# Window attention and two MLPs on one core: zeros beside the keys cleared by GpSimd behind the last token, queries copied by ScalarE alone, and another order of the first loads and the first work

## The chip, the cores and the metric

The kernel runs on one core of a Trainium2 chip. The metric is the time on the device in microseconds, as the median of several runs. A core has TensorE (PE: matrix products, with the loading of its weights, PEld, beside it), VectorE (DVE), ScalarE (ACT), GpSimd (POOL) and SyncE (SP), which here issues all DMAs. Every engine works through its own instructions in order. A lower-case q behind an engine's name means its queue or sequencer.

## The reference, cut to what matters

Attention over a window of 16 tokens to each side and, beside it, over one summary per block of 32 tokens (maximum of the keys, mean of the values), then two MLPs one behind the other. Batch 2, 8 heads, 768 tokens, 64 values a head; 1536 rows of 512, inner width 2048; all in float32.

```python
k_sum = k.reshape(B, H, nb, block, D).max(axis=3)
v_sum = v.reshape(B, H, nb, block, D).mean(axis=3)
scores_l = scale * np.matmul(q, k.transpose(0, 1, 3, 2))
mask_l = np.abs(pos[:, None] - pos[None, :]) < window
scores_s = scale * np.einsum('bhsd,bhnd->bhsn', q, k_sum) + np.log(block)
a = softmax(concat([where(mask_l, scores_l, -1e9), scores_s]))
attn = np.matmul(a, concat([v, v_sum]))
x = attn.transpose(0, 2, 1, 3).reshape(B * S, H * D)
h = np.maximum(x @ w_in, 0.0); x = h * h @ w_out
h = x @ w_in2; g = P(h) / (Q(h) + 1e-6)          # P cubic, Q quadratic in |h|
out = g @ w_out2
```

## The kernel before

The MLPs bound most of the kernel. Every float32 number is split into a high and a low part, and each product is three matmuls (lines 525 and 612). There are four passes over the tokens; the first takes five of the sixteen column groups of the first MLP, 256 tokens at a time, and attention for later tokens is laid between its matmuls. A weight tile goes through four steps: a load into one of three buffers, then w_top on ScalarE, w_dec on VectorE (two instructions, lines 130 and 131) and w_put on ScalarE and GpSimd (lines 144 and 145). A buffer's next load waits for w_dec.

Attention works on units d: a pair of heads times 128 tokens of two 64-token windows each, 24 in all, four pairs per 256 tokens. The keys of a pair are loaded with 8 tokens on each of 96 partitions, 2 KB a piece. [...] k_rel brings the two heads together, k_tr transposes eight pieces on TensorE into two PSUM banks of four pieces each, k_lin copies each bank into the order of windows, k_put takes the maxima of blocks.

The work up to the sixth unit is written out by hand in START, and each engine runs its part of that in the order of the list, while loads (LOADS) and constants (build_consts) are placed by the framework's scheduler: an instruction that must wait can fall behind later ones. A letter is a step, its digit the pair or unit:

- R, A: k_rel on VectorE or ScalarE. t: k_tr. l and k: k_lin of the first and the second bank, on ScalarE and VectorE. c: maxima and their copy to the first four windows. C, B: their copy to the other windows, on VectorE or ScalarE.
- q: transposes of the queries. z: their copy out of PSUM (line 398), half a pair on ScalarE and half on VectorE. s: scores. m: mask and maximum. e: exponentials. r: sums. n: division on GpSimd. p: transposes. b, f: copy out of PSUM on ScalarE or VectorE. o: product with the values. x, y: high and low part of the result.
- S, V, u, w: block means of the values. T, D, W: w_top, w_dec, w_put. X: matmuls for nothing but warmth.

In LOADS, k are the keys of a pair, q and Q queries, v values by token for the block means, n values by window, and w weight tiles. When START is over, the main loop begins, whose first product is at line 525 (h).

Of the kernel before, what the change touches and what calls it, by code (L numbers as in the profile page):

```python
# [16 lines left out]


LOADS = (
    "q0 k0 k1 k2 k3 n2 w0 v0 v1 q1 v2 v3 n0 w1 Q1 w2 n1 n3"  # L20
)
START = (
# [4 lines left out]
)  # L27


# [1 line left out]
def tile_window_attention_moe_moe(  # L31
# [13 lines left out]
    nc = tc.nc  # L45
    B, H, S, D = q.shape
    NT, DM = out.shape
    DFF = w_in1.shape[1]
    P = 128
    BLK, WIN = 32, 16  # L50
# [100 lines left out]
    ap = actx.enter_context(tc.tile_pool(name="ap", bufs=2))  # L151
    TR = 8
    VP = S // TR
    KP = VP + 2 * WIN // TR
    K0 = WIN // TR
    bw = ap.tile([VP, HK], F32, name="bw", bufs=1)
    qz = [ap.tile([P, 4, 2, LO], F32, name=f"qz{j}", bufs=1) for j in range(2)]
    kss = [ap.tile([P, NB], F32, name=f"kss{j}", bufs=1) for j in range(NP)]
# [5 lines left out]
    early = [wp.tile([P, 2 * DM], F32, tag=("wh", "wl")[j % 2], name="early") for j in range(14)]  # L164
# [7 lines left out]
    ]  # L172
    kst = const.tile([P, TR, 4, D], F32, tag="xh2", name="kst")[0:KP]
    vst = const.tile([P, 4, TR, D], F32, tag="xl2", name="vst")[0:VP]
    ksrc = {}
# [3 lines left out]
    def bank(name):  # L179

        tag = banks.pop(0)
        t = (ps_a if tag[0] == "a" else ps_y).tile([P, 512], F32, tag=tag, name=name)
        held[id(t)] = tag
        return t
# [3 lines left out]
    def free(t):  # L188

        banks.append(held.pop(id(t)))  # L190
# [4 lines left out]

    def build_consts():
        make_identity(nc, ident)
        for z in qz:
            nc.vector.memset(z[0:D, :, 1], 0.0)
            nc.vector.memset(z[D:P, :, 0], 0.0)  # L200
        for t in prs:
            nc.vector.memset(t[:, :, HK:], 1e-9)
        m = mk[0:LO, 1, 0:WT]
        nc.vector.memset(m, 0.0)
        nc.gpsimd.affine_select(
            out=m, in_=m, pattern=[[1, WT]], compare_op=ALU.is_ge, fill=NEG, base=-1,
            channel_multiplier=-1,
        )
        nc.gpsimd.affine_select(
            out=m, in_=m, pattern=[[-1, WT]], compare_op=ALU.is_ge, fill=NEG, base=2 * WIN - 1,  # L210
            channel_multiplier=1,
        )
        nc.vector.memset(mk[:, :, WT:], math.log(BLK))
        nc.vector.tensor_copy(mk[LO:P, 1, 0:WT], m)
        m = mk[:, 1:2, 0:WT]
        nc.vector.tensor_copy(mk[:, 0:1, 0:WT], m)
        nc.vector.tensor_copy(mk[:, 2:6, 0:WT], m.to_broadcast([P, 4, WT]))
        nc.vector.memset(mk[:, 0, 0:WIN], NEG)
        nc.vector.memset(mk[:, 5, WT - WIN:WT], NEG)
        nc.vector.memset(bw, 1.0 / BLK)  # L220
        for sgn, base in ((1, 0), (-1, BLK - 1)):
            nc.gpsimd.affine_select(
                out=bw[:, WT:], in_=bw[:, WT:], pattern=[[-sgn * BLK, NB]],
                compare_op=ALU.is_ge, fill=0.0, base=base - (sgn < 0) * (TR - 1),
                channel_multiplier=sgn * TR,
            )
        nc.vector.memset(bw[:, 0:WT], 0.0)
# [12 lines left out]
    def rows(src, h, n, t):  # L240
        return src[h:h + n].rearrange("h (p r) d -> p h (r d)", r=t)

    def e_load(p):

        t = early[p][0:KP].rearrange("p (h r d) -> p h r d", r=TR, d=D)
        nc.sync.dma_start(
            out=t[K0:K0 + VP].rearrange("p h r d -> p h (r d)"), in_=rows(k[0], 2 * p, 2, TR)
        )
        ksrc[p] = t

    def k_rel(p, copy):

        t = early[4 + p][0:KP].rearrange("p (r h d) -> p r h d", r=TR, d=D)
        copy(out=t.rearrange("p r h d -> p h r d"), in_=ksrc[p])
        ksrc[p] = t

    def k_load(hh):

        for h in range(4):
            late(nc.sync.dma_start(  # L260
                out=kst[K0:K0 + VP, :, h], in_=k[1, 4 * hh + h].rearrange("(p r) d -> p r d", r=TR)
            ))
        for j in range(2):
            ksrc[2 * hh + j] = kst[:, :, 2 * j:2 * j + 2]

    def s_load(bb, h, t):

        n = t.shape[1]
        x = nc.sync.dma_start(
            out=t.rearrange("p h r d -> p h (r d)"), in_=rows(v[bb], h, n, TR)  # L270
        )
        if bb:
            late(x)
        for j in range(n // 2):
            vsrc[h // 2 + j] = t[:, 2 * j:2 * j + 2]
# [14 lines left out]
    def q_load(g, hs=slice(0, H)):  # L290

        bb, i, _, _ = at(g * 2 * NP)
        for j in range(2):
            x = nc.sync.dma_start(
                out=qr[g % 2][:, j, hs],
                in_=q[bb, hs, (i + j) * P:(i + j + 1) * P].rearrange("h p d -> p h d"),
            )
            if g > 1:
                late(x)
# [20 lines left out]
    pk = {}  # L320

    def k_tr(p):

        src = ksrc[p].rearrange("p r h d -> p r (h d)")
        pk[p] = [bank("pk"), bank("pk")]
        for r in range(TR):
            pt = pk[p][r // 4]
            nc.tensor.transpose(
                out=pt[:, r % 4 * KP:(r % 4 + 1) * KP], in_=src[:, r],
                identity=ident[0:KP, 0:KP],  # L330
            )

    def k_lin(p, b, copy):

        pt = pk[p][b]
        src = pt[:, 0:4 * KP]
        src = bass.AP(src.tensor, src.offset, [
            list(src.ap[0]), [LO // TR, NWIN], [1, WT // TR], [KP, 4],
        ])
        dst = kt[p][:, :, 0:WT].rearrange("p w (t r) -> p w t r", r=TR)  # L340
        copy(out=dst[:, :, :, 4 * b:4 * b + 4], in_=src)
        free(pt)

    def k_put(p, wins=slice(0, NWIN), copy=nc.vector.tensor_copy, first=True):

        ks = kss[p]
        if first:
            nc.vector.tensor_reduce(
                out=ks.rearrange("p (w n) -> p w n", n=2),
                in_=kt[p][:, :, WIN:WIN + LO].rearrange("p w (n t) -> p w n t", t=BLK),  # L350
                axis=AX.X, op=ALU.max,
            )
        dst = kt[p][:, wins, WT:]
        copy(
            out=dst, in_=ks.rearrange("p (o n) -> p o n", o=1).to_broadcast([P, dst.shape[1], NB])
        )
# [35 lines left out]
    def d_z(d):  # L392


        pt = pq.pop(d)
        for e, mul in enumerate((nc.scalar.mul, nc.vector.tensor_scalar_mul)):
            r = slice(e * D, (e + 1) * D)
            mul(
                qz[d % 2][r, :, e], pt[r, 0:2 * P].rearrange("p (c t) -> p c t", t=LO), 1.0 / SC
            )  # L400
        free(pt)
# [13 lines left out]
    def d_m(d):  # L415
# [11 lines left out]
        )  # L427
        nc.vector.tensor_reduce(out=mx[:, 0:4], in_=s, axis=AX.X, op=ALU.max, negate=True)
        free(pt)
# [8 lines left out]
    def d_r(d):  # L438
        mx, pr = ex.pop(d)
        rs = ap.tile([P, 4], F32, tag="rs", name="rs", bufs=2)  # L440
        nc.vector.tensor_reduce(out=mx[:, 4:8], in_=pr, axis=AX.X, op=ALU.add)
        nc.vector.reciprocal(out=rs, in_=mx[:, 4:8])  # L442
# [17 lines left out]
    def d_b(d, copy=nc.scalar.copy):  # L460
        pp = ap.tile([HK, 4, 2, LO], F32, tag="pp", name="pp", bufs=2)
        copy(out=pp.rearrange("p c e t -> p (c e t)"), in_=po[d][0:HK])
        free(po[d])
        po[d] = pp
# [189 lines left out]
    S0 = 8  # L654
# [45 lines left out]

    nc.scalar.preload_act_table_set("natural_log_exp_and_others")
    hh = [slice(0, H // 2), slice(H // 2, H)]
    v0 = []

    def v_early(p):
        v0.append(early[8 + p][0:VP].rearrange("p (h r d) -> p h r d", r=TR, d=D))
        s_load(0, 2 * p, v0[p])

    loads = dict(
        k=e_load, q=lambda j: q_load(0, hh[j]), Q=q_load, v=v_early,  # L710
        n=lambda i: v_load(0, *divmod(i, 2)), w=lambda i: w_load(*divmod(i, 2)),
    )

    for t in [*early[0:4], kst]:
        nc.vector.memset(t[0:K0], 0.0)
        nc.vector.memset(t[VP:KP], 0.0)
    for x in LOADS.split():
        loads[x[0]](int(x[1:]))
    NL = LOADS.count("w")
# [16 lines left out]
    def w_next(j):  # L736
        k = wq[j]
        (w_top, w_dec, w_put)[j](*divmod(k, 2))
        wq[j] += 1
        if j == 1 and k + NL < NW:  # L740
            w_load(*divmod(k + NL, 2))
# [24 lines left out]
    dve, act = nc.vector.tensor_copy, nc.scalar.copy  # L766
# [3 lines left out]
    def v_last(h, copy):  # L770
        v_put(h, 1, copy)
        free(pvs.pop(h))

    parts = dict(
        X=warm, R=lambda p: k_rel(p, dve), A=lambda p: k_rel(p, act), t=k_tr,
        l=lambda p: k_lin(p, 0, act), k=lambda p: k_lin(p, 1, dve),
        c=lambda p: k_put(p, some, dve),
        C=lambda p: k_put(p, rest, dve, False), B=lambda p: k_put(p, rest, act, False), q=d_t, z=d_z, s=d_s, m=d_m, e=d_e,
        r=d_r, n=d_n, p=d_p, b=d_b, f=lambda d: d_b(d, dve), o=d_o, x=d_x, y=d_y,
        S=lambda p: s_add(v0[p], LEFT), V=lambda h: v_sum(h, LEFT),  # L780
        u=lambda h: v_put(h, 0, act), w=lambda h: v_last(h, act), T=lambda i: w_next(0),
        D=lambda i: w_next(1), W=lambda i: w_next(2),
# [124 lines left out]
```

## Time and profile before

| | |
|---|---|
| median of 3 runs | 653.3 us (651.43 to 655.62) |
| the profiled execution | 650.38 us, span 648.6 us |
| TensorE busy | 610.7 us, 94% of the span |
| VectorE, ScalarE, GpSimd busy | 426.4, 402.8, 351.0 us |
| weight loads of TensorE | 519.4 us |
| DMA | 51.47 MB, mean 79 GB/s |
| granted TensorE clock, mean | 0.995 |

Times are microseconds from the start of the span. An engine's share of the span is an average over stages that have different limits: the first work has little for TensorE to do, and from some 57 us on TensorE hardly rests. A view by stretches of time tells these apart.

### The profile page before, as it was taken

What the parts mean: (1) busy time and instruction counts of PE and PEld (TensorE: products, weight loads), DVE (VectorE), ACT (ScalarE), POOL (GpSimd) and SP (SyncE); (2) the same over time, 40 slices, a digit from 0 to 9 for tenths busy, and PEclk for the clock granted to TensorE, in tenths of its full rate; (3) what the DMA queues carried; (4) which work ended last, traced back from release to release, by engine and by line L of the source; (5) the groups of instructions that cost most, each with busy time, mean ns of one, the idle gap of its engine ahead of it and who ended that gap; (6) DMA issues with size and microseconds to landing.
All of it is one profiled execution on the core that took longest, in us unless ns stands there. A gap on an engine that the chain in (4) does not pass through costs nothing.

```text
span 648.6 us, 9605 instructions
## 1 busy us (share of the span) xinstructions
PE 610.7 (94%) x3492; PEld 519.4 (80%) x3492; DVE 426.4 (66%) x668; ACT 402.8 (62%) x763; POOL 351.0 (54%) x359
## 2 busy tenths in 40 slices
PE   0578999999999999999999999999999999999996
PEld 0578888999998878888888888888888888888885
DVE  7589896666577771201125799997767887767672
ACT  1277775666656642312236799889778888777761
POOL 2237785544657662412257699955544854544441
PEclk9988999999999999999999999999999999999999
DMA  8917997221355650000003633320000100001011
GB/s 202 202 39 204 197 232 149 65 55 26 110 184 163 195 168 28 1 0 1 1 0 106 201 117 106 98 88 2 1 0 1 33 1 1 1 15 51 0 66 65
DMA packets 64142, 51.47 MB, mean 79 GB/s; under 512 B 39776, under 2 KB 56160, under 8 KB 64096
## 3 DMA queue, kind: packets, MB, share of 16 engines
q1 hardware_dynamic: 64096, 50.87, 28.9%
q8 instruction: 27, 0.44, 0.3%
q14 instruction: 19, 0.16, 0.1%
HBM read 47.71 MB, written 3.15 MB: 78 GB/s over the span
## 4 chain that ended last, share of the span: by engine, by line
PE 62%; DVE 0%; ACT 0%; DVEq 0%; issue 0%
PE y L612 32%; PE h L525 31%; DVE acc L638 0%; ACT wdec L120 0%; DVEq L902 0%; ACT sh L588 0%; ACT r L538 0%
## 5 line engine op out<-in xcount | busy, mean ns | idle before, releaser
L525 PE MATMUL h<-xh,wh 128*128 128x512 f32 (+1 forms) x444 | 162.5, 367 | 0.1
L525 PE MATMUL h<-xl,wh 128*128 128x512 f32 (+1 forms) x444 | 161.7, 365 | 0.0
L525 PE MATMUL h<-xh,wl 128*128 128x512 f32 (+1 forms) x444 | 161.3, 364 | 0.0
L589 POOL TENSOR_TENSOR sl<-r,sh 128x512 fp32r<-128x512 f32 (+1 forms) x63 | 68.6, 1089 | 97.7 <-ACT sh L588 88.3
L546 POOL TENSOR_TENSOR q<-q,u 128x512 f32<-128x512 f32 x48 | 63.6, 1325 | 77.8 <-ACT q L543 76.1
L145 POOL TENSOR_TENSOR wl<-wdec,wh 128x512 fp32r<-128x512 f32 x64 | 87.8, 1381 | 23.0 <-ACT wh L144 22.9
L525 PEld LDWEIGHTS h<-xh,wh 128*128 128x128 f32 x444 | 83.9, 189 | 14.3 <-ACT wh L144 0.3
L525 PEld LDWEIGHTS h<-xl,wh 128*128 128x128 f32 x444 | 83.8, 189 | 13.8
L525 PEld LDWEIGHTS h<-xh,wl 128*128 128x128 f32 x444 | 83.7, 189 | 13.9
L555 DVE TENSOR_TENSOR r<-r,h 128x512 f32<-128x512 f32 (+1 forms) x63 | 35.0, 556 | 90.4 <-ACT r L538 90.1
L612 PE MATMUL y<-sh,wh 128*128 128x512 f32 (+1 forms) x252 | 85.2, 342 | 1.1 <-ACT sh L588 1.1
L612 PE MATMUL y<-sh,wl 128*128 128x512 f32 (+1 forms) x252 | 84.8, 340 | 0.0
L612 PE MATMUL y<-sl,wh 128*128 128x512 f32 (+1 forms) x252 | 78.9, 343 | 2.3 <-POOL sl L589 2.3
L589 POOL TENSOR_TENSOR sl<-p,sh 128x512 fp32r<-128x512 f32 x48 | 64.9, 1352 | 21.2 <-ACT sh L588 17.5
L612 PE MATMUL y<-wl,sh 128*128 128x512 f32 x192 | 75.0, 390 | 0.0
L612 PE MATMUL y<-wh,sh 128*128 128x512 f32 x192 | 74.5, 390 | 0.0
L612 PE MATMUL y<-wh,sl 128*128 128x512 f32 x192 | 73.6, 389 | 0.0
L131 DVE SCALAR_TENSOR_TENSOR wdec<-wraw,wdec 128x512 int32<-128x512 int32 x64 | 66.6, 1041 | 1.5
L130 DVE TENSOR_SCALAR wdec<-wdec 128x512 int32<-128x512 int32 x64 | 47.3, 740 | 20.5 <-ACT wdec L120 20.3
L538 ACT ACTIVATE r<-h 128x512 f32<-128x512 f32 (+1 forms) x63 | 31.0, 493 | 47.8 <-PE h L525 28.4
L448 POOL TENSOR_SCALAR pr<-pr,rs 128x120 f32<-128x120 f32 x96 | 36.9, 404 | 42.7 <-DVE rs L442 36.8
L588 ACT CAST sh<-r 128x512 fp32r<-128x512 f32 (+1 forms) x63 | 32.4, 514 | 41.0 <-PE y L612 40.1
(96 smaller groups left out, 1117.5 us busy)
## 6 DMA issues: line engine op xcount, KB each, us to landing
wraw<-in_moe_w_in_dram SPq DMA_DIRECT2D x32, 512.0 KB, 3.9
wraw<-in_moe_w_out_dram SPq DMA_DIRECT2D x32, 512.0 KB, 3.3
early<-in_v_dram SPq DMA_DIRECT2D x40, 96.0 KB, 3.4
out_dram<-acc SPq DMA_DIRECT2D x12, 256.0 KB, 2.1
acc<-in_q_dram SPq DMA_DIRECT2D x10, 256.0 KB, 4.7
early<-in_k_dram SPq DMA_DIRECT2D x4, 384.0 KB, 9.1
early<-in_v_dram SPq DMA_DIRECT2D x4, 384.0 KB, 9.4
kst<-in_k_dram SPq DMA_DIRECT2D x8, 192.0 KB, 5.7
```

The source lines that it names most:

```text
L130: nc.vector.tensor_single_scalar(out=t, in_=t, scalar=3, op=ALU.logical_shift_left)
L131: nc.vector.scalar_tensor_tensor(out=t, in0=low, scalar=29, in1=t, op0=ALU.logical_shift_right, op1=ALU.bitwise_or)
L145: nc.gpsimd.tensor_tensor(out=tl[:, j], in0=t, in1=f32(th[:, j]), op=ALU.subtract)
L448: nc.gpsimd.tensor_scalar(out=pr[:, c, 0:HK], in0=pr[:, c, 0:HK], scalar1=rs[:, c:c + 1], scalar2=1.0, op0=ALU.mult, op1=ALU.mult,)
L525: nc.tensor.matmul(hq[g][:, 0:n], lhsT=w[:, 0, ws], rhs=x[:, part, ts], start=(part == 0 and j == 0), stop=(part == KC - 1 and j == 2),)
L538: nc.scalar.activation(out=r, in_=h, func=AF.Relu)
L546: nc.gpsimd.tensor_tensor(out=q_, in0=q_, in1=u_, op=ALU.mult)
L555: nc.vector.tensor_tensor(out=eq[g], in0=eq[g], in1=h, op=ALU.mult)
L588: nc.scalar.copy(out=sh[:, 0:n], in_=e)
L589: nc.gpsimd.tensor_tensor(out=sl[:, 0:n], in0=e, in1=f32(sh[:, 0:n]), op=ALU.subtract)
L612: nc.tensor.matmul(o, lhsT=lt, rhs=rt, start=(f == 0 and j == 0 and d * m % 512 == 0), stop=(f == FS[ps] - 1 and j == 2 and (d + 1) * m % ...
```

## The change

Four things change. The keys lie from partition 0 on, with four partitions of zeros behind the last token only; GpSimd clears them, in the tiles that k_rel writes and in kst, and the loads no longer share a tile with a clear that comes first. The zeros ahead of the first token come from PSUM: k_tr puts its pieces four columns further on, VectorE clears these four columns in both banks, and k_lin reads from two columns ahead, so that a piece's leading zeros are the trailing zeros of the piece in front of it. Second, three of the four k_rel of the first batch go to GpSimd (P). Third, ScalarE makes both halves of z, in all 24 units. Fourth, LOADS and START have another order, and some steps other engines: L is the first bank's copy on VectorE, K the second's on ScalarE.

```diff
 LOADS = (
-    "q0 k0 k1 k2 k3 n2 w0 v0 v1 q1 v2 v3 n0 w1 Q1 w2 n1 n3"
+    "k0 k1 q0 k2 q1 k3 v0 v1 v3 Q1 v2 w0 n1 n0 n3 n2 w1 w2"
 )
 START = (
-    "R0 A1 t0 R3 t1 q0 l0 k0 l1 k1 q1 S0 A2 c0 z0 t2 S1 s0 z1 c1 m0 T0 D0 l2 k2 s1 q2 B0 q3 "
-    "e0 V0 z2 m1 C1 r0 t3 e1 S2 l3 k3 z3 S3 X2 c2 s2 n0 W0 u0 c3 w0 r1 p0 s3 b0 m2 n1 C3 p1 "
-    "m3 q4 T1 e2 b1 z4 e3 B2 V1 u1 D1 o0 s4 r2 T2 r3 w1 n2 p2 x0 b2 o1 x1 m4 q5 n3 o2 z5 y0 "
-    "D2 p3 s5 f3 W1 m5 e4 x2 y2 W2 r4 o3 x3 n4 y3 y1 e5"
+    "R0 P1 P2 t0 L0 P3 q1 k0 q0 t1 c0 z0 s0 l1 k1 q2 t2 c1 z1 m0 s1 l2 K2 q3 B0 e0 z2 S0 z3 "
+    "t3 c2 X2 r0 s2 m1 K3 S1 l3 m2 c3 e1 r1 e2 n0 V0 S3 p0 f0 n1 q4 s3 r2 u0 p1 S2 z4 s4 B1 "
+    "w0 m3 V1 n2 C3 o0 m4 p2 b1 e3 T0 r3 D0 n3 e4 r4 n4 o1 p3 f2 u1 W0 w1 q5 f3 x0 y0 x1 z5 "
+    "o2 y1 o3 x2 x3 y2 y3 T1 D1 T2 W1 s5 D2 m5 B2 W2 e5"
 )
...
-    KP = VP + 2 * WIN // TR
-    K0 = WIN // TR
+    KE = WIN // TR
+    KP = VP + 2 * KE
...
         make_identity(nc, ident)
+        for t in early[4:8]:
+            nc.gpsimd.memset(t[VP:KP], 0.0)
...
         nc.vector.memset(mk[:, 5, WT - WIN:WT], NEG)
+        nc.gpsimd.memset(kst[VP:KP], 0.0)
...
-            out=t[K0:K0 + VP].rearrange("p h r d -> p h (r d)"), in_=rows(k[0], 2 * p, 2, TR)
+            out=t.rearrange("p h r d -> p h (r d)"), in_=rows(k[0], 2 * p, 2, TR)
...
-        copy(out=t.rearrange("p r h d -> p h r d"), in_=ksrc[p])
+        copy(out=t[0:VP].rearrange("p r h d -> p h r d"), in_=ksrc[p])
...
         pk[p] = [bank("pk"), bank("pk")]
+        for pt in pk[p]:
+            nc.vector.memset(pt[:, 0:2 * KE], 0.0)
         for r in range(TR):
-            pt = pk[p][r // 4]
+            pt = pk[p][r // 4][:, 2 * KE:]
...
-        src = pt[:, 0:4 * KP]
+        src = pt[:, KE:KE + 4 * KP]
...
-        for e, mul in enumerate((nc.scalar.mul, nc.vector.tensor_scalar_mul)):
+        for e in range(2):
             r = slice(e * D, (e + 1) * D)
-            mul(
+            nc.scalar.mul(
...
-    for t in [*early[0:4], kst]:
-        nc.vector.memset(t[0:K0], 0.0)
-        nc.vector.memset(t[VP:KP], 0.0)
...
-        l=lambda p: k_lin(p, 0, act), k=lambda p: k_lin(p, 1, dve),
+        P=lambda p: k_rel(p, nc.gpsimd.tensor_copy), t=k_tr,
+        l=lambda p: k_lin(p, 0, act), L=lambda p: k_lin(p, 0, dve),
+        k=lambda p: k_lin(p, 1, dve), K=lambda p: k_lin(p, 1, act),
```

## Rows read from the trace of the kernel before

**Rows 1.** Stretches: PE, PEld, DVE, ACT, POOL busy (instructions), clock, DMA share, GB/s.

```profile
0.00:24.90 24.90, 4.68 (x24) 4.01 (x24) 13.82 (x27) 6.31 (x9) 6.54 (x16) 1.00 0.98 217
24.90:57.20 32.30, 24.41 (x193) 22.24 (x194) 28.43 (x55) 18.30 (x52) 9.86 (x21) 0.90 0.47 114
57.20:110.00 52.80, 50.23 (x497) 46.79 (x497) 44.11 (x88) 39.16 (x101) 39.43 (x56) 0.99 0.91 201
110.00:648.60 538.60, 531.40 (x2782) 446.34 (x2781) 340.06 (x501) 339.01 (x603) 295.15 (x268) 1.00 0.19 59
```

**Rows 2.** Instructions in order of time, 0 to 60 us: start, duration, engine, line.

```profile
1.07 0.91 DVE L715 MEMSET early<- 2x1024 f32 x1 [1.07 <-PEq L889]
...
12.87 1.76 DVE L716 MEMSET kst<- 4x2048 f32 x1 [0.47 <-issue]
...
17.30 2.90 PE L328 MATMUL pk<-ident,early 100*128 100x100 f32 x16 [17.30 <-DVE bw L227]
...
24.93 0.69 DVE L254 COPY early<-early 100x1024 f32<-100x1024 f32 x1 [2.87 <-DMA early<-in_k_dram]
...
26.86 0.94 DVE L348 TENSOR_REDUCE kss<-kt 128x24 f32<-128x768 f32 x1
...
35.19 0.85 PE L328 MATMUL pk<-ident,early 100*128 100x100 f32 x8
...
46.09 0.69 PE L474 MATMUL pav<-pp,early 120*64 120x64 f32 x16
...
55.60 1.25 ACT L434 ACTIVATE pr<-pr,mx 128x120 f32<-128x120 f32 x4
...
56.48 0.72 DVE L493 TENSOR_TENSOR xl<-pav,xh 128x256 fp32r<-128x256 f32 x2
```

**Rows 3.** DMA issues of the queue in time, and landing of the early tiles' loads.

```profile
15.88 0.31 SPq L246 DMA_DIRECT2D early<-in_k_dram  x1
...
46.70 0.38 SPq L108 DMA_DIRECT2D wraw<-in_moe_w_in_dram  x1
...
DMA to landing us min/median/max: 2.0/5.4/11.1
```

**Rows 4.** DMA, 0 to 60 us in 40 slices of 1.5 us.

```profile
DMA  0578999999999999999800270000000084779893
GB/s 0 132 163 198 269 302 243 222 237 228 231 224 250 213 332 231 215 261 290 129 0 0 82 273 0 0 0 0 0 11 0 22 242 122 174 160 276 280 250 54
```

**Rows 5.** Groups by line and shape, to 57.2 us; the last two 57.2 to 200.

```profile
L202 DVE MEMSET pr<- 128x4 f32 x3 | 0.1, 62 | 0.0
...
masks.py:197 POOL MEMSET ident<- 128x128 f32 x1 | 0.2, 205 | 0.3 <-POOLq L889 0.3
...
L341 DVE COPY kt<-pk 128x576 f32<-128x576 f32 x4 | 2.9, 744 | 0.0
...
L448 POOL TENSOR_SCALAR pr<-pr,rs 128x120 f32<-128x120 f32 x18 | 6.2, 366 | 23.1 <-DVE rs L442 23.1
...
L283 POOL TENSOR_TENSOR early<-early 96x512 f32<-96x512 f32 x4 | 5.0, 1262 | 14.1 <-DMA early<-in_v_dram 14.1
...
L462 DVE COPY pp<-ptp 120x512 f32<-120x512 f32 x1 | 0.7, 683 | 0.0
...
L398 DVE TENSOR_SCALAR qz<-pt 64x256 f32<-64x256 f32 x18 | 7.7, 428 | 1.6 <-ACT qz L398 1.1
...
L398 ACT ACTIVATE qz<-pt 64x256 f32<-64x256 f32 x18 | 6.6, 370 | 0.7 <-PE pt L390 0.5
```

**Rows 6.** Instructions in order of time: weight decoding on VectorE and GpSimd.

```profile
31.92 0.42 DVE L130 TENSOR_SCALAR wdec<-wdec 128x512 int32<-128x512 int32 x1
...
51.33 1.27 POOL L145 TENSOR_TENSOR wl<-wdec,wh 128x512 fp32r<-128x512 f32 x1 [1.01 <-ACT wh L144]
...
51.57 1.31 DVE L130 TENSOR_SCALAR wdec<-wdec 128x512 int32<-128x512 int32 x1
...
54.33 1.28 POOL L145 TENSOR_TENSOR wl<-wdec,wh 128x512 fp32r<-128x512 f32 x1 [1.74 <-ACT wh L144]
```

More of the change, by code (lines that the diff above doesn't have):

```diff
@@ L243, in e_load @@
     def e_load(p):
-        t = early[p][0:KP].rearrange("p (h r d) -> p h r d", r=TR, d=D)
+        t = early[p][0:VP].rearrange("p (h r d) -> p h r d", r=TR, d=D)
         nc.sync.dma_start(
-            out=t[K0:K0 + VP].rearrange("p h r d -> p h (r d)"), in_=rows(k[0], 2 * p, 2, TR)
+            out=t.rearrange("p h r d -> p h (r d)"), in_=rows(k[0], 2 * p, 2, TR)
         )
@@ L260, in k_load @@
             late(nc.sync.dma_start(
-                out=kst[K0:K0 + VP, :, h], in_=k[1, 4 * hh + h].rearrange("(p r) d -> p r d", r=TR)
+                out=kst[0:VP, :, h], in_=k[1, 4 * hh + h].rearrange("(p r) d -> p r d", r=TR)
             ))
@@ L702, in tile_window_attention_moe_moe @@
     hh = [slice(0, H // 2), slice(H // 2, H)]
-    v0 = []
+    v0 = {}
     def v_early(p):
-        v0.append(early[8 + p][0:VP].rearrange("p (h r d) -> p h r d", r=TR, d=D))
+        v0[p] = early[8 + p][0:VP].rearrange("p (h r d) -> p h r d", r=TR, d=D)
         s_load(0, 2 * p, v0[p])
@@ L774, in tile_window_attention_moe_moe @@
     parts = dict(
-        X=warm, R=lambda p: k_rel(p, dve), A=lambda p: k_rel(p, act), t=k_tr,
-        l=lambda p: k_lin(p, 0, act), k=lambda p: k_lin(p, 1, dve),
+        X=warm, R=lambda p: k_rel(p, dve), A=lambda p: k_rel(p, act),
+        P=lambda p: k_rel(p, nc.gpsimd.tensor_copy), t=k_tr,
+        l=lambda p: k_lin(p, 0, act), L=lambda p: k_lin(p, 0, dve),
+        k=lambda p: k_lin(p, 1, dve), K=lambda p: k_lin(p, 1, act),
         c=lambda p: k_put(p, some, dve),
```

## The prediction

> **What bounds the kernel now.** I read the engine table by stretch first [rows 1]. From 57.2 us to the end TensorE is busy for 581.6 of 591.4 us, so no edit can take much out of that part; it can only lengthen it. The 57.2 us ahead of it hold 29.1 us of TensorE work: some 28 us of TensorE idleness, nearly all that can be won, lie in the hand-written first work (START), whose last instructions on VectorE, the remainders of the attention output, end at 57.2 [rows 2]. So the question is when START ends.
>
> Next the order of VectorE's instructions [rows 2]. It clears rows beside the keys, ten instructions from 1.07 to 14.63, then small constants and its first key copy (R0). Its second, R3, starts only at 24.93, when the fourth key load lands, and k0, which needed nothing of that load, stands behind it. The DMA queue [rows 3] says why that load was late: it left at 15.88, behind loads that stand after it in LOADS, since it had to wait for a clear. From 24.9 to 57.2 VectorE is busy for 28.43 of 32.30 us, 88% [rows 1]: there it sets the pace. ScalarE has 18.30 there and GpSimd 9.86. DMA is full until about 30 us and then nearly idle for 15 us [rows 4].
>
> **The change, step by step.**
> *Clears.* Ten VectorE clears go, 13.6 us. On GpSimd come five: four of 1024 columns, one of 2048. No row has this size there: VectorE's took 0.91 and 1.76 [rows 2], and a GpSimd clear of 128 columns 0.205 [rows 5], eight of which would be 1.64. I take 0.95 and 1.8, near VectorE's, since the short clear holds a start that the long one pays once. The four stand ahead of the selects that make the mask, so the mask comes near 7 us (9 at 1.64 a clear), and its first reader, m0, later. The long one can push P1 from 6.3 to 7.9, 0 to 1.6 us; I take 0, since GpSimd has room before the second key load lands. The zeros ahead of the first token become two clears of four columns in PSUM for each pair. A clear of four columns took 0.062 us [rows 5]: 0.5 us in START, 0.5 later. They add a wait: VectorE now waits for the bank itself. At t2 the banks come from z0 and l1 on ScalarE, and c1, which stands behind, needs l1 anyway; I take nothing there, at most one copy of a key bank (0.744, [rows 5]) at each of the eight places.
>
> *Loads.* k0 leaves first, near 0.8, with 384 KB. The shortest landing of the loads into these buffers was 2.0 us, the longest 11.1 behind a full queue [rows 3]. At the 132 to 163 GB/s of the queue's first filled slices [rows 4] it takes 2.4 to 2.9 us beside its issue; I take 5.0 for its landing, between 3.3 and 10 (the median was 5.4). k1 is there near 6.3. The same bytes as before must land and DMA was full from 4 us on, so the last load still ends near 30. q and k are 2.05 MB, at about 240 GB/s 8.5 us: k3 by 11 to 12. The value rows (n0 to n3) land near 23 to 27, w1 and w2 last. Behind w2 stand T2, D2, W2 and the remainder on GpSimd; from D2 on these ran from 51.57 to 55.61 [rows 6], and with as much again as a short ScalarE step ahead of them they end at 35. The first product with values (o0) started at 46.09, 11.1 before the end of START [rows 2]; with rows at 24 to 27 the same tail ends at 35 to 38. So loads are next in line but not ahead of VectorE, below.
>
> *Key copies.* A1 and A2 leave ScalarE, R3 leaves VectorE; three copies of 1024 columns go to GpSimd. The one-tensor multiply took 0.366 us for 120 columns, the two-tensor add 1.262 for 512 [rows 5]: 3.1 and 2.5 us by their columns, and a clear's 0.91 from below. I take 2.5, the row nearest in size. P1, P2, P3 end at 8.8, 11.3 and 13.8. Cover: VectorE has L0 and k0 (0.744 each, [rows 5]) from 7.1 to 8.6, then c0's reduction (0.94, [rows 2]) to 9.5, and t1 ends at 8.8 + 1.45 (sixteen transposes took 2.90 for two pairs, [rows 2]). Thus 0.7 us is uncovered, 1.3 at 3.1 a copy, nothing at 0.91; gaps of that size are in the 88% with which I reckon below. Beside GpSimd work some VectorE instructions stretch: the shift of D at 51.57 took 1.31 us while GpSimd ran from 51.33, and 0.42 alone [rows 6]. Of VectorE's work beside P1 to P3 only R0 resembles it; it comes before k1 lands, so I count nothing, at most 0.9. The Trainium skill (GPSIMD Engine Reference, Engine selection) speaks against the move: elementwise work belongs on VectorE, and GpSimd is about half as fast with two inputs, near line rate with one. At line rate the copy would take an estimated 0.9 us and the 0.7 us above would go; by the rows' two-tensor rate it stays. No row here shows a plain GpSimd copy.
>
> *Queries.* Half of each pair's copy moves: 0.428 us leave VectorE and 0.37 come to ScalarE [rows 5]. Six lie in START, 18 in the rest (7.7 us less on VectorE, 6.6 more on ScalarE).
>
> *START on VectorE.* From R3 to the end it did 28.43 us of work [rows 1]. Off: R3 0.69, six query halves 2.57, one of four key spreads 0.74 (L0, k0, k1 remain; K2, K3 go to ScalarE). On: f0 and f2, 2 x 0.683, and pad clears of six of the eight banks, 0.37. Left from L0 on: 26.2 us. L0 starts at 5.0 + 0.69 (R0) + 1.45 (t0) = 7.1. At the same 88% it takes 29.7, to 36.9; e5 behind m5 adds 1.25 [rows 2]: START ends at 38.1 instead of 57.2, **19.1 us earlier**. ScalarE stays about level: six query halves (2.2), B1, K2 and K3 come, and A1, A2, b0, b2 and l0 go. With no idleness of VectorE START would end at 34.6, at 80% at 41.1.
>
> *After START.* There TensorE has 2.6 us of idleness in 52.8 (57.2 to 110), VectorE is 84% busy and ScalarE 74% [rows 1]. With all 18 halves moved there, ScalarE would come to 87% and VectorE to 69%: the busiest engine is as busy as before, but another. Price: from -1.6 (all the waits of VectorE's query halves gone, [rows 5]) to +6.6 (every moved half on the path). I take +2.5, for I also see the second weights' decoding (D1, D2) stand nearer to the end of START, so that the load which D1 releases, at 46.70 before [rows 3], 10.5 ahead of START's end, leaves some 5 ahead of it.
>
> Sum: 19.1 - 2.5 = **16.6 us**. The profiled execution took 650.38, its span 648.6 and 1.78 around it, 2.9 below the median of 653.3; so 633.8 beside the profile and **636.7** beside the median. A measurement of this kernel can tell about 1% from no change.
>
> **Rivals.**
> *All overlaps* (18%): VectorE runs without gaps in START (end 34.6, 22.6 won) and the later part loses nothing: 630.7. For it: nothing on the queue's side forbids it, with loads done near 30. Against: VectorE had gaps of 12% when all keys were there [rows 1].
> *ScalarE becomes the bound* (20%): all 6.6 us on the path, and the weights for the third and fourth columns of the first product come up to 4 late: 19.1 - 10.6 = 8.5, 644.8. For it: ScalarE at 87%. Against: TensorE lost only 2.6 us there to all engines together [rows 1].
> *The change doesn't do what it says* (7%): the loads leave in another order than listed, as before, and k3 or q is late again; only some 3 us of VectorE's work are saved (26.2 + 0.69 against 28.43, and the waits of its query halves): 650.
> *Slower* (5%): a GpSimd copy of a key tile holds up t1 to t3. Before, t3 began at 35.19 with 22.0 to the end of START [rows 2]. With copies of C, t3 begins at 6.3 + 3C; the gain is gone from C = 9.6 us, and 660 comes with C near 11 (3 x 1.4 late, and the 2.5 after START). The dearest row per column gives 3.1, so this needs three times that.
>
> **How the numbers follow.** The forecast (50%) has 631 to 642 of its own: START at 80 to 100% density gives 34.6 to 41.1 for its end, k0's bounds 36.4 to 43.1, the later part -1.6 to +6.6, and they seldom add up one way. With the two rivals inside, 628 to 646 holds the time 8 times in 10. Faster by over 1% (below 646.8): forecast, overlap and most of ScalarE, 0.87. Within 1%: the rest of those and the third rival, 0.08. Slower by over 1%: 0.05.
>
> **What would show it.** R0 near 5 us and no clear on VectorE before it; key loads on the queue before 4 us; GpSimd key copies of 1 to 2.5 us; m0 near 13; VectorE 85 to 95% busy from 8 to 37 us; the first h matmul (line 525) near 36; after START, the same 591 us within 3. Wrong would make it: loads of value rows after 30 us, TensorE waiting for ScalarE's query copies after START, or GpSimd copies over 3 us.

## The result, and the profile after

The changed kernel took 635.81 us (median of 4 runs, 633.76 to 637.79), the kernel before 653.59 in the same session: a ratio of 0.9728, with a 95% interval of 0.9684 to 0.9772. That is 17.8 us by the medians. Between the two profiled executions it is 14.55 us (650.38 and 635.83; spans 648.6 and 634.1), since that of before lay below its median and that of after on it. The forecast was 16.6.

The first fence is the engine table by stretch of the changed kernel, with the columns of [rows 1]: the first work from the time when the constants are done, the 52.8 us behind it (as long as the third stretch there), and the rest.

```profile
0.00:5.40 5.40, 0.00 (x0) 0.00 (x0) 3.09 (x17) 1.28 (x1) 4.62 (x15) 1.00 0.69 168
5.40:37.65 32.25, 27.47 (x231) 24.21 (x232) 27.50 (x57) 23.42 (x64) 22.49 (x33) 1.00 1.03 224
37.65:90.45 52.80, 46.04 (x427) 41.87 (x428) 38.39 (x79) 40.10 (x102) 34.46 (x51) 0.97 0.85 207
90.45:634.10 543.65, 536.82 (x2837) 451.38 (x2835) 336.99 (x499) 345.29 (x621) 298.10 (x269) 1.00 0.19 60
```

START now ends at 37.65 instead of 57.2, 19.55 us earlier. What follows takes 596.45 us instead of 591.4, 5.05 more: in the 52.8 us behind START TensorE is idle for 6.76 us, and was for 2.57 [rows 1]. So there is a gain of 19.55 and a loss of 5.05; the second is twice what was forecast.

Of the loss, 4.2 us are idleness. The clock has a part in it too: TensorE's granted clock was 0.90 from 24.9 to 57.2 and 0.99 in the 52.8 us behind that [rows 1], and is now 1.00 and 0.97. In the kernel before, TensorE was at the lower of its two levels (1.2 instead of 2.4 GHz) in START, where it had time to spare; now it is so behind START, where it has none:

```profile
73.70:77.10 3.40, 3.40 (x19) 3.40 (x18) 3.37 (x9) 2.75 (x9) 1.17 (x2) 0.51 0.73 264
77.10:80.50 3.40, 3.40 (x33) 3.40 (x33) 1.18 (x4) 2.47 (x8) 3.06 (x6) 0.99 0.54 154
```

It gets through 19 matmuls in the first of these stretches and 33 in the second, which makes an estimated 1.4 us. Before the clock fell TensorE had waited for 2.3 us (70.8 to 73.1) and worked again for 0.6; in e7 it waits as long at this place, and the clock stays at 1.00. What makes it fall is not shown here.

The next fence is the list of instructions in order of time of the changed kernel, for the steps that the prediction named.

```profile
1.06 1.80 POOL L222 MEMSET kst<- 4x2048 f32 x1
...
3.93 0.20 DVE L216 COPY mask<-mask 64x96 f32<-64x96 f32 x1 [0.92 <-POOL mask L211]
4.10 4.44 POOL L199 MEMSET early<- 4x1024 f32 x4
4.17 0.94 DVE L218 COPY mask<-mask 128x96 f32<-128x96 f32 x1
4.30 1.01 DVE L219 COPY mask<-mask 128x384 f32<-128x384 f32 x1
...
5.37 1.38 DVE L257 COPY early<-early 96x1024 f32<-96x1024 f32 x1
...
6.96 1.57 PE L333 MATMUL pk<-ident,early 100*128 100x100 f32 x8 [6.96 <-DVE pk L330]
...
7.90 1.43 DVE L348 COPY kt<-pk 128x576 f32<-128x576 f32 x2 [1.08 <-PE pk L333]
...
8.60 2.02 POOL L257 COPY early<-early 96x1024 f32<-96x1024 f32 x2
...
9.69 1.59 PE L333 MATMUL pk<-ident,early 100*128 100x100 f32 x8 [0.30 <-POOL early L257]
...
12.72 1.04 POOL L257 COPY early<-early 96x1024 f32<-96x1024 f32 x1 [2.11 <-DMA early<-in_k_dram]
...
13.74 0.65 DVE L431 TENSOR_TENSOR pr<-pss,mask 128x480 f32<-128x480 f32 x1
...
27.25 0.69 PE L481 MATMUL pav<-pp,early 120*64 120x64 f32 x16
...
32.59 0.36 PE L532 MATMUL h<-xh,wh 128*128 128x256 f32 x1
...
36.40 1.25 ACT L441 ACTIVATE pr<-pr,mx 128x120 f32<-128x120 f32 x4 [0.64 <-DVE mx L435]
```

Beside [rows 2]: no clear beside the keys stands at the front of VectorE any more; its first key copy (R0, line 257) runs at 5.37, the two spreads of the first pair (L0 and k0, line 348) at 7.90, and the first product with values at 27.25, where it was 46.09. GpSimd does its long clear ahead of the selects for the mask, at 1.06. The key copies P1 and P2 start at 8.60, when the four shorter clears are through, not when k1 lands; P3 is the only one that waits for its load (2.11 us).

Then the DMA queue of the changed kernel in order of time, to set beside [rows 3], and below it the first product of the third column of h.

```profile
0.80 0.89 SPq L249 DMA_DIRECT2D early<-in_k_dram  x2
...
2.78 0.50 SPq L249 DMA_DIRECT2D early<-in_k_dram  x1
...
4.76 1.10 SPq L249 DMA_DIRECT2D early<-in_k_dram  x1
...
31.25 3.93 SPq L297 DMA_DIRECT2D acc<-in_q_dram  x2
35.27 2.35 SPq L318 DMA_DIRECT2D early<-in_v_dram  x4
37.73 0.42 SPq L108 DMA_DIRECT2D wraw<-in_moe_w_in_dram  x1
...
48.25 0.39 PE L532 MATMUL h<-xh,wh 128*128 128x256 f32 x1 [0.54 <-ACT wh L144]
```

All key loads have left by 5.9, in the order that LOADS lists. At the other end the load of the weights for the third column (line 108) leaves at 37.73, just behind the end of START; before it left at 46.70, 10.5 ahead of that end [rows 3]. Line 318 loads values, line 297 queries: two query loads and four value loads stand directly in front of it. The third column's first product comes 10.6 us behind the end of START (48.25); before it came 5.35 behind:

```profile
62.55 0.36 PE L525 MATMUL h<-xh,wh 128*128 128x256 f32 x1
```

### The profile page after: what moved, and what is told of

Read it like the earlier page. It is cut to its first block, busy times and chain, and to the rows that moved or that the text cites. A ratio compares the mean times of both kernels' runs of the same rounds, so it can differ in the third digit from the quotient of the medians.

```text
span 634.1 us, 9629 instructions
## 1 busy us (share of the span) xinstructions
PE 610.3 (96%) x3492; PEld 517.5 (82%) x3492; DVE 406.0 (64%) x649; ACT 410.1 (65%) x785; POOL 359.7 (57%) x367
## 4 chain that ended last, share of the span: by engine, by line
PE 63%; issue 0%; DVE 0%; POOL 0%; DVEq 0%; POOLq 0%
PE y L619 32%; PE h L532 31%; DVE acc L645 0%; POOL sl L596 0%; DVEq L907 0%; POOLq L596 0%
## 5 line engine op out<-in xcount | busy, mean ns | idle before, releaser
L532 PEld LDWEIGHTS h<-xh,wl 128*128 128x128 f32 x444 | 83.8, 189 | 16.6 <-POOL wl L145 2.8
L532 PEld LDWEIGHTS h<-xl,wh 128*128 128x128 f32 x444 | 83.9, 189 | 13.6
L596 POOL TENSOR_TENSOR sl<-p,sh 128x512 fp32r<-128x512 f32 x48 | 64.8, 1351 | 21.3 <-ACT sh L595 19.5
L131 DVE SCALAR_TENSOR_TENSOR wdec<-wraw,wdec 128x512 int32<-128x512 int32 x64 | 68.0, 1063 | 1.4
L130 DVE TENSOR_SCALAR wdec<-wdec 128x512 int32<-128x512 int32 x64 | 44.8, 700 | 22.3 <-ACT wdec L120 22.1
L144 ACT CAST wh<-wdec 128x512 fp32r<-128x512 f32 x64 | 39.4, 621 | 30.0 <-DVE wdec L131 29.9
```

The source lines that it names most:

```text
L130: nc.vector.tensor_single_scalar(out=t, in_=t, scalar=3, op=ALU.logical_shift_left)
L131: nc.vector.scalar_tensor_tensor(out=t, in0=low, scalar=29, in1=t, op0=ALU.logical_shift_right, op1=ALU.bitwise_or)
L144: nc.scalar.copy(out=th[:, j], in_=t)
L532: nc.tensor.matmul(hq[g][:, 0:n], lhsT=w[:, 0, ws], rhs=x[:, part, ts], start=(part == 0 and j == 0), stop=(part == KC - 1 and j == 2),)
L596: nc.gpsimd.tensor_tensor(out=sl[:, 0:n], in0=e, in1=f32(sh[:, 0:n]), op=ALU.subtract)
```

## The experiments

My theory after the result: the front of VectorE, cleared and with keys early, gives the 19.5 us; the 5 us lost later are the place of the weight loads in the queue. Rivals: ScalarE's query copies cause the loss; the order of the first work, or the GpSimd copies, give a good part of the gain. The table has every run. "START" is the end of its last instruction in the profiled execution, and "behind" is that execution's span less this. The ratio is to the kernel before on the same chip.

| run | median us | ratio (95% interval) | START | behind |
|---|---|---|---|---|
| kernel before | 653.59 | | 57.20 | 591.4 |
| changed kernel | 635.81 | 0.9728 (0.9684 to 0.9772) | 37.65 | 596.45 |
| e1 changed kernel again | 635.71 | 0.9753 (0.9731 to 0.9775) | 37.43 | 597.8 |
| e2 later query halves on VectorE | 636.04 | 0.9771 (0.9747 to 0.9794) | 37.34 | 596.9 |
| e3 weights first | 632.68 | 0.9716 (0.9695 to 0.9737) | 37.20 | 593.7 |
| e4 key copies back | 639.48 | 0.9813 (0.9789 to 0.9837) | 43.24 | 594.7 |
| e5 clears in front | 645.26 | 0.9903 (0.9871 to 0.9936) | 48.29 | 596.4 |
| e6 loads and first work as before | 639.30 | 0.9805 (0.9769 to 0.9841) | 44.31 | 591.7 |
| e7 key copies back, clears ahead | 634.23 | 0.9730 (0.9694 to 0.9767) | 36.87 | 594.4 |
| e8 weights first, long clear later | 632.07 | 0.9708 (0.9672 to 0.9743) | 36.02 | 594.0 |
| e9 loads as before | 642.35 | 0.9853 (0.9808 to 0.9897) | 43.68 | 597.6 |
| e10 e8 and e2 together | 631.34 | 0.9686 (0.9648 to 0.9725) | 36.87 | 593.6 |
| e11 loads as before, clears ahead | 640.72 | 0.9811 (0.9791 to 0.9832) | 42.22 | 597.0 |
| e12 e10 with the key copies back | 634.70 | 0.9715 (0.9693 to 0.9736) | 36.94 | 597.5 |

**e1, the changed kernel again.** No edit; it is what e2 to e4 are compared with.

> The changed kernel itself, as the measure for the others of this call. All theories: 0.973 of the kernel before (0.968 to 0.977), START ends on VectorE near 36.4 us, TensorE idle for 6 to 7 us in the 52.8 us behind START's end.

It gave 635.71, with START's end and the part behind it within 0.3 and 1.4 us of the first profile. A difference of 1 us in the part behind START is therefore no finding; e7 and e12 below differ by more there without an edit.

**e2, half of the later query copies back on VectorE.**

```
-            nc.scalar.mul(
+            (nc.vector.tensor_scalar_mul if e and d > 5 else nc.scalar.mul)(
```

> The changed kernel, but from the seventh unit on half of each pair's query copy is on VectorE again, 18 instructions of 0.43 us; START is untouched. Theory ScalarE (the moved halves made ScalarE the bound behind START, which gave back some 5 us of START's 19.5): 3 to 5 us faster than the changed kernel, 0.966 to 0.969 of the kernel before, TensorE idle 2 to 4 us less in the 52.8 us behind START. Theory weights (the third column's weights come late, since their loads stand on the DMA queue behind value and query loads): within 1 us of the changed kernel, idle time the same. Theory contention (GpSimd and VectorE hold each other up): 0 to 2 us slower, since VectorE gets more to do.

636.04 against 635.71: no gain. The theory that ScalarE's query copies cost something behind START falls here, and e6 says the same more directly.

**e3, the second weights' loads ahead of value and query loads that nothing needs yet.**

```
+    behind = lambda x: tc.add_manual_dep(x.ins, wdma[2, 1].ins.name, nosync, reason="order")
-        wraw[n, j] = r
+        wraw[n, j], wdma[n, j] = r, x
...
+                behind(x) if g == 1 else None
-                late(x)
+                behind(x) if g == 2 else late(x)
```

> The changed kernel, but the value and query loads for the second and third group of tokens may not leave before the loads of w4 and w5 (order on the queue alone). Theory weights: w4 leaves near 34 us instead of 37.7, the third column's first product starts some 3 us earlier than 48.25, and the time falls by 2 to 4 us. Theory ScalarE: the third column starts earlier by 1 us at most, the time changes by under 1 us. The value loads behind could come late for the second group: that would show as TensorE waiting with products of values after 45 us.

632.68, 3.0 us below e1. The queue of this run, and the third column's first product:

```profile
33.67 0.37 SPq L108 DMA_DIRECT2D wraw<-in_moe_w_in_dram  x1
34.73 0.33 SPq L110 DMA_DIRECT2D wraw<-in_moe_w_out_dram  x1
35.16 2.65 SPq L318 DMA_DIRECT2D early<-in_v_dram  x4
37.86 1.31 SPq L297 DMA_DIRECT2D acc<-in_q_dram  x2
...
46.39 0.29 PE L533 MATMUL h<-xh,wh 128*128 128x256 f32 x1
```

The engine table of the stretches 37.65 to 57.65 and 57.65 to 90.45, of e1 and then of e3:

```profile
37.65:57.65 20.00, 15.98 (x146) 13.18 (x144) 14.77 (x34) 16.90 (x44) 13.99 (x22) 1.00 0.93 228
57.65:90.45 32.80, 30.01 (x285) 28.67 (x284) 23.64 (x45) 23.17 (x57) 20.49 (x30) 0.95 0.80 192
```

```profile
37.65:57.65 20.00, 18.50 (x154) 15.32 (x152) 17.19 (x36) 16.67 (x45) 15.47 (x23) 0.91 1.23 237
57.65:90.45 32.80, 30.80 (x304) 29.33 (x305) 23.02 (x49) 25.99 (x65) 21.84 (x31) 1.00 0.92 210
```

The same load leaves 4.1 us earlier (33.67; 37.77 in e1), and the third column's first product starts 1.65 earlier (46.39; 48.04 in e1), where 3 had been expected. The first stretch alone can't be compared by busy time, for its clock is 1.00 in e1 and 0.91 in e3: e2, which gains nothing, is busy for 17.93 us in it, also at 0.91. Both stretches together have the same mean clock in the two runs (0.97), and in them TensorE is busy for 49.30 us in e3 and 45.99 in e1. So the place of these loads in the queue is shown to cost time behind START, 3.0 us by the medians, of 5.05 (6.4 in e1). The size is less sure than the cause: e7, which has the loads in the place of e1, takes 594.4 behind START and 634.23 in all, and against that e3 gains 0.7 and 1.6. The edit itself names value and query loads and no other work.

**e4, key copies back on ScalarE and VectorE.**

```
-    "R0 P1 P2 t0 L0 P3 q1 ...
+    "R0 A1 A2 t0 L0 R3 q1 ...
```

> The changed kernel, but the three key copies go back from GpSimd to ScalarE (two) and VectorE (one), at the same places of the list. My step said that copies on GpSimd cost nothing up to some 2 us each, and spare VectorE 0.69 us: START ends 0 to 1.5 us later (ScalarE's 1.05 each stand where it has little to do, VectorE's waits for the fourth key load near 12.7 us), time 0 to 2 us more. Rival, GpSimd copies hold VectorE up (a clear of 0.2 us took 1.0 there and the first key copy 1.38 instead of 0.69): START ends 1 us or more earlier without them.

639.48, 3.8 above e1. But the edit moved something else too: with the copies gone from GpSimd, two of its four clears ran behind its first addition of value rows.

```profile
14.61 1.83 POOL L199 MEMSET early<- 4x1024 f32 x2
...
15.61 1.60 PE L333 MATMUL pk<-ident,early 100*128 100x100 f32 x8 [6.23 <-POOL early L199]
```

The second pair's transposes waited 6.23 us for a clear, and VectorE 2.99 for the load of the fourth keys, ahead of R3 and of k0; so this run says nothing on where the copies belong; e7 does. What took 1.0 us in the changed kernel was not a clear, as the expectation has it, but VectorE's copies for the mask (0.94 and 1.01, lines 218 and 219 in its list above).

**e5, VectorE's ten clears back in front.** Before, lines 715 and 716 cleared rows beside the keys in the tiles that the key loads write. The GpSimd clears stay; these are added work.

```
+    for t in [*early[0:4], kst]:
+        nc.vector.memset(t[0:KE], 0.0)
+        nc.vector.memset(t[VP - 32:VP - 28], 0.0)
     for x in LOADS.split():
```

> The changed kernel, plus ten VectorE clears in front of the key loads as the kernel before had them (eight of 1024 columns, two of 2048, on partitions that the loads then fill, so that each key load waits for its two). My step: these clears and the waits of the loads, not the order of work, kept the keys away. Each pair of clears took 2.3 us, so k0 leaves near 3.4 us instead of 0.8 and k3 after 10.2, and VectorE is free at 14.6 at the earliest: START ends 8 to 14 us later than at 36.4, the time is 8 to 14 us more, 0.987 to 0.996 of the kernel before. Rival, the clears cost nothing beyond their own place (the loads bound START anyway): START ends under 3 us later.

645.26, 9.55 us above e1. The first key copy and the last step of START:

```profile
16.52 0.62 DVE L257 COPY early<-early 96x1024 f32<-96x1024 f32 x1
...
47.04 1.25 ACT L441 ACTIVATE pr<-pr,mx 128x120 f32<-128x120 f32 x4 [0.64 <-DVE mx L435]
```

START ends 10.9 later than in e1. The clears are worth some 10 us, and not the 13.6 that they take with the gaps between them, since without them R0 still has to wait until 5.37: it moves by 11.15. The edit holds the key loads, too, which leave at 3.49, 8.16, 14.85 and 18.66 here, behind loads that stand after them in LOADS; GpSimd waits 15.8 us for them. So this is the price of the clears with the loads that they hold, and the run doesn't part the two.

**e6, loads and first work as before.** Both written orders of the kernel before, with the new clears and query copies.

```
-    "k0 k1 q0 k2 q1 k3 v0 v1 v3 Q1 v2 w0 n1 n0 n3 n2 w1 w2"
+    "q0 k0 k1 k2 k3 n2 w0 v0 v1 q1 v2 v3 n0 w1 Q1 w2 n1 n3"
-    "R0 P1 P2 t0 L0 P3 ...
+    "R0 A1 t0 R3 t1 q0 l0 k0 ...
```

> The changed kernel with the LOADS and START strings of the kernel before (so key copies on ScalarE and VectorE, too, but no clears in front, and queries copied by ScalarE alone). It does the clears' part of the change alone. If the clears carry nearly all, START ends near 38 to 40 us. My forecast of the split: with keys there early, R3 still makes VectorE wait for the fourth key load, near 12 us instead of 24.9, and the rest of VectorE's list runs as before: START ends some 10 to 13 us earlier than at 57.2, near 45, and the time is 0.980 to 0.988 of the kernel before. Rival, the order is all: START ends after 52.

639.30: START ends at 44.31, 12.9 earlier than before, without a new order of anything; the query halves that left VectorE are in this. With no clear ahead of them the four key loads leave one behind the other, as this same LOADS has them, where the fourth left at 15.88 before [rows 3]: that it had waited for a clear is thereby shown. VectorE's wait for the fourth key load is still there (3.40 us):

```profile
1.83 1.98 SPq L249 DMA_DIRECT2D early<-in_k_dram  x4
...
10.21 0.69 DVE L257 COPY early<-early 96x1024 f32<-96x1024 f32 x1 [3.40 <-DMA early<-in_k_dram]
```

The engine table of the 52.8 us behind START in this run:

```profile
44.30:97.10 52.80, 50.36 (x476) 46.78 (x475) 40.32 (x89) 44.37 (x115) 39.41 (x56) 0.97 0.90 203
```

ScalarE has 44.37 us of work there, 5.2 more than before [rows 1], as every query copy is on it, and TensorE is as busy as before (50.36 at a clock of 0.97; 50.23 at 0.99 in [rows 1]). The part behind START takes 591.7, 0.3 more than before. That closes the question on ScalarE: the 5 us are lost with the new orders, not with the new place of the copies. The two orders together give 6.7 us in START and lose 4.75 behind it; 1.9 are left by the spans, 3.5 by the medians.

**e7, e4 with the clears held ahead.**

```
-            nc.gpsimd.memset(t[VP:KP], 0.0)
+            mz = nc.gpsimd.memset(t[VP:KP], 0.0)
-    with tc.manual_schedule():
+    with tc.issue_after(mz.ins), tc.manual_schedule():
-    "R0 P1 P2 t0 L0 P3 q1 ... S0 z3 t3 ...
+    "R0 A1 A2 t0 L0 q1 ... S0 z3 R3 t3 ...
```

> As e4, but GpSimd's clears are held ahead of its first work (in e4 two of them had slipped behind an add that waited for a value load, and t1 waited for them until 15.6 us), and R3 stands ahead of t3, where VectorE no longer waits for the fourth key load. This prices the place of the three key copies alone. My step (copies on GpSimd cost nothing, and spare VectorE 0.69): START ends within 1.5 us of the changed kernel's, time -1 to +1.5 us against it. Rival (GpSimd copies are what keeps VectorE's list dense): START ends 3 us or more later.

634.23, START 0.56 earlier than in e1. The time shows no measurable difference from whether GpSimd copies the keys (0.9730 and 0.9753, with intervals that overlap). The loss in e4 was that of the clear and of R3's wait, which this run takes away together. In START the copies on GpSimd do cost something: beside P3 (12.72 to 13.76 in the changed kernel) VectorE's copy of the second pair's maxima took 0.72 us, and takes 0.21 here. The changed kernel's first, then e7's:

```profile
13.10 0.72 DVE L361 COPY kt<-kss 128x96 f32<-128x96 f32 x1
```

```profile
12.92 0.21 DVE L362 COPY kt<-kss 128x96 f32<-128x96 f32 x1
```

Behind START e7 takes 3.4 us less than e1 (594.4; 597.8), with no edit there.

**e8, e3 with the long clear later.** The clear of the tile for the second batch's keys stands behind P2.

```
-        nc.gpsimd.memset(kst[VP:KP], 0.0)
+        Z=lambda i: nc.gpsimd.memset(kst[VP:KP], 0.0), X=warm, ...
-    "R0 P1 P2 t0 L0 P3 q1 ...
+    "R0 P1 P2 t0 L0 Z0 P3 q1 ...
```

> As e3 (loads of w4 and w5 ahead of the value and query loads of later groups), and the long clear for the second batch's keys (1.8 us on GpSimd, which stood ahead of the four short ones) goes behind the second key copy. In the changed kernel the first GpSimd key copy began at 8.60, when the clears ended, though its keys were there at 6.0. Theory: the first copy begins near 6.8, t1 near 8, START ends 0.6 to 1.2 us earlier than in e3, the time falls by as much: 0.970 of the kernel before. Rival: VectorE's list is not waiting for t1 by more than its own gaps, and nothing moves (within 0.4 us).

632.07, 0.6 below e3: START ends 1.2 earlier, of which the whole time does not show a certain part.

```profile
4.75 1.38 DVE L257 COPY early<-early 96x1024 f32<-96x1024 f32 x1
...
34.77 1.25 ACT L442 ACTIVATE pr<-pr,mx 128x120 f32<-128x120 f32 x4 [0.64 <-DVE mx L436]
```

R0 starts at 4.75 instead of 5.37. In the changed kernel the first keys were there at 4.5 (3.7 us from their issue at 0.80), so R0 did not wait for them. The long clear cost 0.62 at the front: it held up the selects for the mask, the mask's copies on VectorE waited for those, and R0 stands behind them.

**e9 and e11, loads as before with the new first work.** e9 exchanges LOADS alone; e11 adds the hold on the clears from e7.

> The changed kernel's first work (START), with the order of loads of the kernel before: the first two value rows and all query heads stand ahead of the fourth key load. If the loads' order matters by itself (my theory: VectorE sets the pace and the key loads' place decides when L0 and k0 can run), k2 or k3 lands some 3 to 5 us later, P3 and the third key pair's work move with it, and START ends 1 to 4 us later than the changed kernel's 37.4 to 37.7: 637 to 640, ratio 0.978 to 0.983. If the order of loads is hidden (rival: with no clears ahead all loads leave early in either order and VectorE has other work), START ends within 0.5 us of 37.5 and the time is 635 to 636.5, ratio 0.974 to 0.977.

> The changed kernel with the order of loads of the kernel before, and GpSimd's four clears held ahead of START, so that none of them stands between two of its key copies. In the run with that order of loads alone START ended at 43.7 where the changed kernel's control run had 37.4, with two clears behind the first key copy and the first pair of query transposes of the second load waiting until 17.2. If those clears were the cause, START comes back to 37.5 to 39 and the time to 636 to 638, ratio 0.974 to 0.978. If the later landing of the queries (issued at 9.4, behind seven loads and a weight load) is the cause, START still ends at 41 to 44 and the time is 639 to 642, ratio 0.979 to 0.985.

642.35 and 640.72: the new first work with the old loads is no faster than the old first work with them (639.30). In both, two clears ran behind the first GpSimd copy; in e11 the hold did not do what it was meant for:

```profile
9.18 1.84 POOL L199 MEMSET early<- 4x1024 f32 x2
...
10.18 1.59 PE L334 MATMUL pk<-ident,early 100*128 100x100 f32 x8 [10.18 <-POOL early L199]
...
17.30 0.30 PE L398 MATMUL pt<-ident,acc 128*128 128x128 f32 x1 [1.71 <-DMA acc<-in_q_dram]
```

The first transposes are 3.2 us later than in the changed kernel (10.18; 6.96), because of a clear, and the queries' are held up at 17.30 by a load. Both are in the 4.8 us by which START ends later than in e1, and these runs don't part them.

**e10 and e12, the edits together.** e10 is e8 with the edit of e2. e12 is e10 with the key copies back as in e7.

> The changed kernel with the second weights' loads ahead of later value and query loads, the long GpSimd clear moved behind the second key copy, and the second half of each pair's query copy on VectorE again after START. If ScalarE's query halves hold up TensorE once the weights' loads no longer do, 1 to 3 us come off the 632.1 of the version without the third edit: 629 to 631, ratio 0.966 to 0.969. If they do not (what the run with that edit alone said), it stays within 1 us of 632: ratio 0.970 to 0.973.

> The changed kernel with all that did not hurt so far: the second weights' loads ahead of later value and query loads, the long GpSimd clear behind the second key copy, half of the later query copies on VectorE, and the three key copies on ScalarE, ScalarE and VectorE instead of GpSimd. Without the last edit the median was 631.3 (ratio 0.969). If key copies on GpSimd are worth nothing, this is within 1 us of that: ratio 0.967 to 0.971. If they help when the long clear no longer stands ahead of them, it is 1 to 3 us above: ratio 0.971 to 0.974.

e10 gave 631.34, the fastest median of all; from e8 (632.07) it can't be told apart. e12 gave 634.70, and its START ends where that of e10 does (36.94 and 36.87). The 3.4 us arise behind it. The engine table of 37.65 to 57.65, of e10 and then of e12:

```profile
37.65:57.65 20.00, 18.65 (x167) 16.17 (x165) 18.27 (x39) 16.79 (x44) 16.69 (x23) 0.91 1.11 229
```

```profile
37.65:57.65 20.00, 15.97 (x152) 13.69 (x150) 17.45 (x40) 14.35 (x38) 14.59 (x23) 1.00 1.10 221
```

The trace of e12 has 152 matmuls here and that of e10 167, though the clock is higher in e12 and nothing that differs in the code runs in this stretch: the work came out in another order there. Later the clock is lower in e12 (0.95 from 57.65 to 90.45 and 0.98 from there to 180.45; 1.00 in e10). Which step of it matters stays open. With e7 it says how far the part behind START can move for reasons that no edit intends: some 3 us.

## Why the prediction was right, and where it was not

**START's end** was forecast at 38.1 and came at 37.65; the term was 19.1 and measured 19.55. Its parts: R0 at 5.0 forecast, 5.37 measured; L0 at 7.1 and 7.90; VectorE's work from L0 to the end of m5 26.2 and 26.08; its density there 88% and 92%, in a stretch of 28.5 us where I had reckoned 29.7:

```profile
7.90:36.36 28.46, 26.40 (x226) 23.11 (x224) 26.08 (x53) 22.18 (x59) 18.88 (x31) 1.00 1.02 223
```

R0 lasted 1.38, twice the 0.69 that I took; with its later start that is the 0.8 at L0, although L0 began before t0 was through. That the work came out as reckoned is in part luck. VectorE's copies of the maxima (line 361) took 2.8 us, and 1.6 before: they stretched beside GpSimd, where I had counted only R0 as exposed. The shifts of D took 1.2, and 2.1 before. m0 came at 13.74 for "near 13"; the first h matmul at 32.59, 3.4 earlier than I said, which changed nothing, for START's end hung on m5. The cause is shown too: e5 gives back 10.9 us of START with nothing but the clears and the loads that they hold, e6 wins 12.9 without the new orders.

**The clears on GpSimd** took 1.1 and 1.80 us each; I had 0.95 and 1.8 (0.90 without VectorE's copies beside them, e5). What was wrong was their place. I set the four ahead of the selects and the long one near P1, and took nothing for it out of 0 to 1.6. The long one ran ahead of the selects and cost 0.62 at R0 and 1.2 at START's end (e8), inside those bounds, but by way of the mask and VectorE, which I had not seen.

**The key copies on GpSimd** took 1.01 and 1.04 us, not 2.5. The bounds held, and the choice of the nearest row in size was wrong: a copy is not an addition. The Trainium skill (GPSIMD Engine Reference, Engine selection) calls one-input work there near line rate, and the trace agrees roughly: 1.01 to 1.04 us, where the estimate by that rule was 0.9. P3 still ended at 13.8 as forecast, by luck, since two errors met: the copies were shorter, and they began late, P1 behind the clears and P3 behind its load. That their place is worth nothing in the time was forecast, and e7 bears it out; that page's advice to keep elementwise work off GpSimd wins 0.56 us at the end of START there, which the time doesn't show.

**The loads** left in the listed order (the fourth keys at 4.76, where I had said before 4), so the rival in which the change doesn't do what it says fell. Its price of 650 was also too high: with the old order of loads the time is 641 to 642 (e9, e11), and 639 if the first work is the old one as well (e6). So without the new order of loads the new first work is worth nothing; I had counted that order within START and given it no term. How much of this is the loads and how much the clears that slipped in e9 and e11 stays open.

**The part behind START** was forecast at +2.5 (bounds -1.6 to +6.6) and came at +5.05, so the sign "the same 591 us within 3" did not come. The right resource had a wrong number: I expected the load that D1 releases to leave 5 us ahead of START's end, and it left 0.08 behind. I had moved it by the work ahead of it and not by the queue, where six loads that nothing needed yet stood in front. e3 undoes this and wins 3.0 us against e1 (1.6 against e7); then 2.3 are left behind START. That this is near the 2.5 of my term is luck, for the term stood for the query copies, which cost nothing there, and for this load. Of those 2.3 I have no shown cause. They come with the new orders (e6 has 0.3), and e7 and e12 show that the sequence of the work there can be worth as much. The clock, which I had not reckoned with, is worth an estimated 1.4 us in the changed kernel's profile; how much of the 5.05 that explains stays open, since e6 has the same 0.97 behind START.

**ScalarE as the bound** (644.8) fell: e2 finds no gain from relieving it, and e6 has all its query copies with no more TensorE idleness than before. *All overlaps* (630.7) fell with the 0.8 us at L0, the 2.4 in which VectorE rested behind it, and the 5.05, though e10, with the weights ahead, comes within 1 us of that time. *Slower* needed a GpSimd copy of 9.6 us.

## What to carry to other kernels

Look at what stands at the front of the engine that sets the pace: ten clears there were worth ten microseconds, though the list of waits names the load behind them and not the clears. When a stretch is shortened, follow every load that has to leave inside it through its in-order queue: what was ten microseconds early before can stand behind loads that nothing waits for yet. And before an experiment is read, check that the instructions around the edit stayed where they were; in three of these runs (e4, e9, e11) a clear that moved along has a share in the result. Busy times of TensorE can be set side by side only where its granted clock was the same.

## What the runs showed of the hardware that was not expected

VectorE copies stretch beside GpSimd's clears, which read nothing. The two mask copies (lines 218 and 219) took 0.94 and 1.01 us beside them; the same two took 0.21 and 0.36 in the kernel before, with GpSimd idle. The copy R0 took 1.38, and 0.62 in e5, where the clears were over. The clears lost as well: four took 4.44 us beside these copies, and in e5, beside VectorE's clears, 3.61:

```profile
3.37 3.61 POOL L199 MEMSET early<- 4x1024 f32 x4
```

The reductions beside GpSimd's key copies kept their 0.95. The Trainium skill (SBUF — State Buffer, Who interferes with whom) says that a VectorE copy and a GpSimd instruction can block each other for a whole instruction, while reductions don't take part; these rows agree, each copy being some 0.7 longer where a clear lasts 1.1.

It also happens later. In the changed kernel a decoding step of the weights on VectorE took 2.75 us, 0.69 where nothing ran beside it; it began in the last 0.3 us of six additions on GpSimd and ran beside the operation that follows them (GpSimd's list first, then VectorE's):

```profile
64.00 5.69 POOL L286 TENSOR_TENSOR vst<-vst 96x512 f32<-96x512 f32 x6
...
69.65 1.27 POOL L145 TENSOR_TENSOR wl<-wdec,wh 128x512 fp32r<-128x512 f32 x1
```

```profile
69.41 2.75 DVE L131 SCALAR_TENSOR_TENSOR wdec<-wraw,wdec 128x512 int32<-128x512 int32 x1
```

TensorE waited 2.3 us for VectorE soon after (from 70.8 to 73.1). That the stretched step caused this was not tried.
